# Tokens gathered in quarter rows and transposed on VectorE, with single-pass list products, in a fused delta-rule attention and expert kernel

## The chip, the core and the metric

The kernel runs on one core of a Trainium2 chip. Five engines work side by side, each through its own instructions in order: TensorE (PE in the profile, its weight loads as PEld), VectorE (DVE), ScalarE (ACT), GpSimd (POOL) and SyncE (SP), which here issues DMA transfers. GpSimd issues the indirect transfers, those whose rows are named by a list of indices. The metric is the device time of one execution in microseconds (us).

## The reference

A linear attention with the delta rule runs over 4 batches and 8 heads, 768 steps, 48 features. Its output, 3072 tokens of 8 x 48 = 384 features, is the input of a mixture of 8 experts: every token goes to the one expert with the highest logit, through two matrices (384 x 1024 and 1024 x 384) with a relu between, and is scaled by its softmax weight.

```python
for t in range(S):
    kt, vt, bt = (k_n[:, :, t], v[:, :, t], beta[:, :, t, None])
    y[:, :, t] = np.einsum('bhd,bhde->bhe', q[:, :, t], state)
    v_old = np.einsum('bhde,bhd->bhe', state, kt)
    state = state + bt[:, :, :, None] * np.einsum('bhd,bhe->bhde', kt, vt - v_old)
...
x = np.ascontiguousarray(attn_out.transpose(0, 2, 1, 3)).reshape(B * S, H * D)
...
logits = x @ w_gate + modality_bias[modality_id]
e_idx = np.argmax(logits, axis=1)
...
for e in range(E):
    mask = e_idx == e
    h = np.maximum(x[mask] @ w1[e], 0.0)
    out[mask] = gate_w[mask, None] * (h @ w2[e])
```

## The kernel before

**Two stages.** The attention stage takes about the first 265 us. Its order is written out by hand: a table of task numbers (`ORDER`, with `FILL`) says in which sequence the plan's tasks are issued, and each engine keeps that order. The attention output goes tile by tile (128 tokens x 384 features) into `xd` in device memory. The router's work and the first slot's loads are tasks of the same plan. Everything behind is written in the order of the program, and a scheduler of the framework, with its own costs, places it on each engine.

**Slots.** Tokens are sorted by expert into slots: a0 and a1 (512 tokens each, taken from the first 16 tiles of 128 tokens, so that they can start before the attention is done), b0, b1 and b2 (512 each, from all that is left), c0 and c1 (256) and e0 (128): 25 tiles. "Later slots" are a1 to e0, 21 tiles. Further slots stand behind a branch for inputs that need them. List a holds the token places of a0 and a1, list b those of the rest.

**Lists** (`Router.lists`, L675 to L710). For four token tiles at a time VectorE writes a one-hot matrix of a token's place within its group of 128 (L633) and a matrix of 0 or 1 that says in which group the token stands (L690), multiplied once by the gate weight (L691) and once by the token's number (L692). TensorE adds the products over all tiles (L698): 16 columns by group and kind for list a, 34 for list b. These are plain fp32 matmuls, which the profile records as two each. From the sums come the token numbers `gidx`, the gate weights and the output rows `sidx` (L700 to L710). List b is made while TensorE works on slots a0 and a1.

**A slot** has these steps. `weights`: eight loads by SP, four quarters of w1 and four of w2 (384 KB each, L793), into buffers that rotate. Each is split into a high part (ScalarE, L824) and a low part, the remainder (VectorE, L828). `tokens`, for each tile of 128: an indirect DMA on GpSimd brings 128 rows of 384 features (L797) into one of five buffers (tag "xs"), three TensorE transposes bring features onto partitions (L800), ScalarE writes the high part xh (L802) and VectorE the low part xl (L803). There is one xh and one xl for all slots: they can be written only when layer 1 of the slot before is done with them. `layer1` (L837): 72 products of 128 x 128 with up to 512 tokens (three terms: high by high, high by low, low by high), relu on ScalarE (L841), low part of h on VectorE (L843). `layer2` (L892): 24 products for each token tile, scaled by the gate on VectorE into one of three output buffers (L895), then an indirect DMA on GpSimd that scatters the 128 rows into the output (L896).

The program writes layer 1 of a slot, then loads and tokens of the next, then layer 2 of the slot; the scheduler mixes them. Tiles carry their slot's name: `xgb_0` is the gathered tile 0 of a b slot, `hpb` layer 1 and `opb` layer 2 of a b slot, `tpb` the sums of list b.

## Time and profile before

| | |
|---|---|
| runs shown | 508.93, 517.02, 517.77 us; median 517.02 |
| profiled execution | 507.84 us |
| its span in the profile | 506.1 us |
| mean granted TensorE clock | 0.944 |
| TensorE busy | 474.1 us (94%) |
| VectorE busy | 318.4 us (63%) |
| ScalarE busy | 200.2 us (40%) |
| GpSimd busy | 121.2 us (24%) |

The profile records one execution; busy time is the sum of an engine's instructions, and the granted clock is the share of full speed that TensorE was given. The span leaves out 1.7 us of the execution around it. Two of the three runs lie about 9 us above the third and the profiled one. In the rows quoted later, "L892 PE MATMUL out<-in" is an operation at line 892 on TensorE, "x16" is the number of records in a piece of the chain, and "[19.44 <-DVE tf2b L709]" is the idle time before it and what ended it.

### The profile page before, as it was taken

The page shows a single profiled execution, that of the slowest core. Times are in us where ns is not written, and L with a number is a line of the kernel's source. Part 1 is how long each engine was busy: PE and PEld are TensorE (multiplying, and loading weights), DVE is VectorE, ACT ScalarE, POOL GpSimd, SP SyncE. Part 2 cuts the span into 40 slices and gives each one's busy share as a digit, 9 for nine tenths or more (in the row PEclk, how much of TensorE's full clock was granted, in tenths as well). Part 3 has the DMA queues.
Part 4 walks back from the last instruction along what each step waited for, and adds up shares of the span by engine and source line. Part 5 has one row for each costly group of instructions (what it writes and reads, how often), then busy time and mean ns, then how long its engine had stood idle before and what let it go on. Part 6 is the DMA issues. An engine that isn't in the chain of part 4 may idle for free.

```text
span 506.1 us, 16393 instructions
## 1 busy us (share of the span) xinstructions
PE 474.1 (94%) x6973; PEld 433.2 (86%) x6973; DVE 318.4 (63%) x668; ACT 200.2 (40%) x396; POOL 121.2 (24%) x158
## 2 busy tenths in 40 slices
PE   6789999999998999899989999999999999999991
PEld 6689999998888888798977898898898898999991
DVE  2598645779788787495666787645355364447650
ACT  3413323536246573452552343224343333335540
POOL 9111420344512212103403020064133030020110
PEclk8589956999999999999989999999999999999996
DMA  8558203518776785575657215157326245146710
GB/s 287 184 148 236 65 3 96 146 55 272 273 198 153 218 279 178 151 213 170 184 181 245 67 62 188 62 157 228 101 94 209 73 139 162 45 132 208 252 64 8
DMA packets 81331, 78.27 MB, mean 155 GB/s; under 512 B 48041, under 2 KB 71607, under 8 KB 79968
## 3 DMA queue, kind: packets, MB, share of 16 engines
q1 hardware_dynamic: 78048, 67.49, 44.8%
q0 software_dynamic: 3200, 9.64, 5.7%
q8 instruction: 57, 0.93, 0.8%
q14 instruction: 26, 0.21, 0.1%
...
## 4 chain that ended last, share of the span: by engine, by line
PE 82%; DMA 6%; DVE 4%; issue 3%; ACT 2%; SPq 1%; POOL 0%; POOLq 0%; DVEq 0%; ACTq 0%
PE hpb L837 10%; PE opb L892 9%; PE opa L892 7%; PE hpa L837 5%; PE lv L390 5%; PE gp L184 4%; PE y L440 3%; PE hpc L837 3%; PE opc L892 3%; PE z L423 3%; PE S L429 3%; PE ks L417 3%; PE S L500 3%; PE y L437 2%; PE jo L314 2%
## 5 line engine op out<-in xcount | busy, mean ns | idle before, releaser
L892 PE MATMUL opb<-w2hb,h 128*128 128x384 f32 x192 | 52.8, 340 | 0.5 <-DVE oob L895 0.5
L843 DVE SCALAR_TENSOR_TENSOR h<-hpb,h 128x512 fp32r<-128x512 f32 x24 | 16.6, 691 | 41.5 <-ACT h L841 41.5
L837 PE MATMUL hpb<-xh,w1xb 128*128 128x512 f32 x144 | 40.7, 394 | 0.0
L892 PEld LDWEIGHTS opb<-w2hb,h 128*128 128x128 f32 x192 | 34.8, 188 | 1.8 <-DVE oob L895 1.0
L892 PE MATMUL opa<-w2ha,h 128*128 128x384 f32 x128 | 34.4, 343 | 0.0
L841 ACT ACTIVATE h<-hpb 128x512 fp32r<-128x512 f32 x24 | 14.4, 598 | 48.0 <-PE hpb L837 48.0
L892 PE MATMUL opb<-w2lb,h 128*128 128x384 f32 x96 | 32.5, 338 | 0.0
L837 PEld LDWEIGHTS hpb<-xh,w1xb 128*128 128x128 f32 x144 | 26.8, 188 | 4.5
L334 POOL TENSOR_TENSOR tmx<-T,A 128x456 f32<-128x456 f32 (+10 forms) x20 | 14.5, 725 | 65.3 <-DVE T L335 64.7
...
L419 DVE TENSOR_TENSOR RHS<-vv,ks 64x384 f32<-64x384 f32 x44 | 24.2, 551 | 4.7 <-PE ks L417 3.9
L500 PE MATMUL S<-ident 128*128 128x128 f32 x154 | 24.5, 304 | 1.5 <-DVE Sb L26 0.5
L896 POOL DMA_INDIRECT out_dram<-oob,sidxb x12 | 12.4, 1032 | 50.5 <-DVE oob L895 28.2
L25 ACT COPY ZT<-z 64x384 f32<-64x384 f32 x36 | 17.0, 473 | 17.3 <-PE z L423 16.8
L334 DVE TENSOR_TENSOR tmx<-T,A 128x396 f32<-128x396 f32 (+14 forms) x40 | 21.6, 539 | 3.6 <-POOL T L335 2.8
L440 PE MATMUL y<-ZT,pb 128*64 128x96 f32 x384 | 21.9, 259 | 2.0 <-DVE ZT L26 2.0
L892 PEld LDWEIGHTS opa<-w2ha,h 128*128 128x128 f32 x128 | 23.1, 188 | 0.8 <-DVE ooa L895 0.2
L500 PEld LDWEIGHTS S<-ident 128*128 128x128 f32 x154 | 21.0, 210 | 3.2 <-issue 0.7
L184 PE MATMUL gp<-kqr 48*64 48x64 f32 x896 | 17.6, 227 | 5.5 <-DMA kqr<-in_kq_dram 4.0
L423 PE MATMUL z<-RHS,R 128*64 128x96 f32 x384 | 22.2, 260 | 0.1
L335 DVE TENSOR_TENSOR T<-T,tmx 128x396 f32<-128x396 f32 (+14 forms) x40 | 21.2, 529 | 1.4
L892 PE MATMUL opa<-w2la,h 128*128 128x384 f32 x64 | 21.6, 337 | 0.0
...
## 6 DMA issues: line engine op xcount, KB each, us to landing
...
ke<-in_kq_dram SPq DMA_DIRECT2D x10, 512.0 KB, 7.6
...
```

Source lines behind the costliest of these rows:

```text
L25: if n=="scalar": nc.scalar.copy(o,i)
L184: s.I[f"g{c}"]=mm(t[k][o:o+64,64*(4*g+j):64*(4*g+j)+64],l,s.KQ[c][u:u+48,g,x,1] if a else l,start=True,stop=True)
L334: E[s.e].tensor_tensor(o,T[:,:,lo:lo+na,c:c+1].to_broadcast([128,n,na,nb]),X[:,:,c:c+1,c+1:32].to_broadcast([128,n,na,nb]),ALU.mult)
L335: x=T[:,:,lo:lo+na,c+1:32]; E[s.e].tensor_tensor(x,x,o,ALU.subtract)
L390: for p in range(2): b=64*p+32; x=2*j+h; mm(o[b-32:b+32,x],s.YS[i%2][b:b+32,x],R[b:b+32,x,32:64] if i>7 else w0(s.Wn[i//4],i)[b:b+32,4*h+j ...
L419: c,g=divmod(i,2); b=64*p; V.tensor_tensor(s.RHS[g][b:b+64,:,48*p:48*p+48].rearrange("q (h j) c -> q h j c",h=2),s.KV[c,1][b:b+64,g],s.ks[ ...
L423: for h in range(2): mm(s.z[i][64*h:64*h+64,:,j,:],s.R[i%4][:,2*j+h,:],hc(s.RHS[i%2][:,4*h+j,:]),start=True,stop=True)
L440: for p in range(2): mm(s.y[i][64*p:64*p+64,:,j,:],s.PB[i//2][:,8*(i%2)+4*p+j],hc(s.ZT[i%2][:,4*p+j,:]),start=(i<2 and j==0),stop=True,ski ...
L500: for _ in range(fill.get(t["k"],0)): s.nc.tensor.matmul(s.S[1][:,384:512],s.ident,s.ident,start=False,stop=True,skip_group_check=True)
L837: if n in ks: mm=s.nc.tensor.matmul(hp[:,v,:],w[:,k,fs],x[:,k,0:T],start=(n==0),stop=(n==8))
L843: s.nc.vector.scalar_tensor_tensor(hl,hp,0.0,hh.bitcast(F32),ALU.max,ALU.subtract)
L892: mm=nc.tensor.matmul(op,h[:,f%nf,ts_],w[:,f%2,:],start=(n==0),stop=(n==23)); n+=1
```

## The change

Four things are changed.

**Gathers.** For later slots, one gather of 128 rows x 384 features becomes four of 128 rows x 96. `xd` is seen as 12288 rows of 96 features, and the row's index is 4 x token + quarter, with the quarter depending on the partition's group of 32 in a way that puts a token's quarter rows where the transposition wants them. These indices (`x4a`, `x4b`) are made with the lists. a0 keeps the old gather, though both kinds share the new function.

**Transposes.** For later slots VectorE transposes the gathered tile in blocks of 32 x 32 (`turnq`) into another of the five "xs" buffers, in place of three TensorE transposes into PSUM. Features stand on partitions in another order then, so w1 is loaded in that order: four transfers of 32 partitions for a quarter of w1 where one stood.

**Lists.** The list products are single-pass (F32R) with four kinds of column (token number, gate high part, gate low part, mask), 32 columns for list a and 68 for list b. VectorE makes one more product for every four tiles, the gate's split and some small tiles once, and the gate's sum. One more product on TensorE spreads the token numbers over the partitions for the quarter indices. It adds two tasks to the plan, so the numbers in `ORDER` from 888 on shift by two, and "887" becomes "887 888 889".

**Drain.** Behind a slot's last scatter GpSimd gets a drain instruction, ahead of what the scheduler places next.

```diff
-...788d 778 478 ... 885 808 479d 886 827 887 809 482 810...
+...788d 778 478 ... 885 808 479d 886 827 887 888 889 809 482 810...
...
+    def split(s,t0,t1):
+        V=s.nc.vector; g,h=(x[:,t0:t1] for x in (s.gt,s.gh))
+        V.tensor_copy(h.bitcast(F32R),g); V.tensor_tensor(g,g,h,ALU.subtract)
...
-                B=LB[:,z][:,0:H*2*NH].rearrange("q (h b n) -> q h b n",h=H,b=2)
+                B=LB[:,z][:,0:H*4*NH].rearrange("q (h b n) -> q h b n",h=H,b=4)
...
-                V.tensor_tensor(B[:,:,0],ids.unsqueeze(1).to_broadcast([128,H,NH]),bn(pi),ALU.is_equal)
-                G.tensor_tensor(B[:,:,1],B[:,:,0],bn(s.gt),ALU.mult)
-                V.tensor_tensor(B[:,:,0],B[:,:,0],bn(s.tid),ALU.mult)
+                V.tensor_tensor(B[:,:,3],ids.unsqueeze(1).to_broadcast([128,H,NH]),bn(pi),ALU.is_equal)
+                for x,y in ((1,s.gh),(2,s.gt),(0,s.tid)): G.tensor_tensor(B[:,:,x],B[:,:,3].bitcast(F32),bn(y),ALU.mult)
...
-        V.tensor_scalar(gidx,tk,-1.0,0.0,ALU.add,ALU.max)
-        V.tensor_copy(gate,tp[:,1])
+        tg=T([128,NH],"tz"); V.tensor_scalar(tg,tk,-1.0,0.0,ALU.add,ALU.max)
+        V.tensor_tensor(tm,tg.unsqueeze(1).to_broadcast([128,4,NH]),m4.unsqueeze(2).to_broadcast([128,4,NH]),ALU.mult)
+        yield "PE",.25
+        nc.tensor.matmul(r4.rearrange("q a b -> q (a b)"),Lr,tm.rearrange("q b n -> q (b n)"),start=not zeroed,stop=True,skip_group_check=True)
+        yield "DVE",2.0
+        V.tensor_scalar(s.places[u][:,4*o0:4*o0+4*NH].rearrange("q (n b) -> q b n",b=4),r4,4.0,s.qn,ALU.mult,ALU.add)
+        V.tensor_copy(gidx,tg)
+        V.tensor_copy(gate,tp[:,1]); V.tensor_tensor(gate,gate,tp[:,2],ALU.add)
...
-        getattr(s.nc,C.w_q).dma_start(w,(s.w1,s.w2)[l-1][bass.ds(S["e"],1),q].rearrange("o p k f -> (o p) k f"))
+        W=(s.w1,s.w2)[l-1] if l==2 or u=="a0" else s.w1q
+        if W is s.w1q:
+            for r in range(4): getattr(s.nc,C.w_q).dma_start(w[32*r:32*r+32],W[bass.ds(S["e"],1),q,r].rearrange("o j k f -> (o j) k f"))
+        else: getattr(s.nc,C.w_q).dma_start(w,W[bass.ds(S["e"],1),q].rearrange("o p k f -> (o p) k f"))
...
     def gather(s,S,t,xg):
-        s.nc.gpsimd.indirect_dma_start(xg,None,S["x"],bass.IndirectOffsetOnAxis(ap=S["gidx"][:,S["c0"]+t:S["c0"]+t+1].bitcast(U32),axis=0))
+        c=S["c0"]+t; G=s.nc.gpsimd; ix=lambda a,c: bass.IndirectOffsetOnAxis(ap=a[:,c:c+1].bitcast(U32),axis=0)
+        if S["u"]=="a0": G.indirect_dma_start(xg,None,S["x"],ix(S["gidx"],c)); return
+        for b in range(4): G.indirect_dma_start(xg[:,96*b:96*b+96],None,S["x"].rearrange("t (q f) -> (t q) f",q=4),ix(s.router.places[S["l"]],4*c+b))
...
+    def turnq(s,xg,xp): s.nc.vector.transpose(xp.rearrange("q k (b t) -> q b k t",b=4),xg.rearrange("q (b k j) -> q b k j",b=4,k=3))
...
-            xp=env["ps"].tile([128,3,128],F32,name=f"xp{u}_{t}",tag=env["xp"],bufs=env["xpb"])
-            s.turn(xg,xp); s.xhi(t,xp); s.xlo(t,xp)
+            xp=s.A.pa.tile([128,3,128],F32,name=f"xt{u}_{t}",tag="xs",bufs=5)
+            s.turnq(xg,xp); s.xhi(t,xp); s.xlo(t,xp)
...
         X.layer2(S,o[0],o[2],not more)
+        if more:
+            with tc.issue_after(X.put.ins): nc.gpsimd.drain()
```

GpSimd, from the last scatter of slot a0 (`ooa_3_...`) on: gathers of b0 and b1 (L797 before, L820 in the changed kernel) and scatters of a1 (L896, L920). Before:

```order
L896 DMA out_dram<-ooa_3_4993,sidxa 3072x384
L797 DMA xgb_0_5135<-xd,gidxb 128x384
L797 DMA xgb_1_5143<-xd,gidxb 128x384
L797 DMA xgb_2_5151<-xd,gidxb 128x384
L797 DMA xgb_3_5159<-xd,gidxb 128x384
L797 DMA xgb_0_5436<-xd,gidxb 128x384
L797 DMA xgb_1_5444<-xd,gidxb 128x384
L797 DMA xgb_2_5452<-xd,gidxb 128x384
L896 DMA out_dram<-ooa_0_5204,sidxa 3072x384
L896 DMA out_dram<-ooa_1_5234,sidxa 3072x384
```

The same place in the changed kernel; "x4" is the four quarters of a tile:

```order
L920 DMA out_dram<-ooa_3_5044,sidxa 3072x384
L820 DMA xgb_0_5199<-xd,x4b 128x96 x4
L920 DMA out_dram<-ooa_0_5272,sidxa 3072x384
L820 DMA xgb_1_5208<-xd,x4b 128x96 x4
L920 DMA out_dram<-ooa_1_5302,sidxa 3072x384
L820 DMA xgb_2_5217<-xd,x4b 128x96 x4
L920 DMA out_dram<-ooa_2_5332,sidxa 3072x384
L820 DMA xgb_3_5226<-xd,x4b 128x96 x4
L920 DMA out_dram<-ooa_3_5362,sidxa 3072x384
L820 DMA xgb_0_5517<-xd,x4b 128x96 x4
```

The four gathers of b0 stood in a row ahead of a1's scatters; now each tile's quarters are followed by a scatter of a1, and the gathers of b1 have moved behind all of them.

TensorE, from the product of the changed kernel's list b that makes the quarter indices (L716) on, in layer 2 of a1 (L916):

```order
L916 MATMUL opa_1_5277<-w2la_3_5159,h_4616 128x384
L716 MATMUL tpb<-l1b 128x68
L916 MATMUL opa_0_5247<-w2ha_3_5158,h_4616 128x384
L916 MATMUL opa_1_5277<-w2ha_3_5158,h_4616 128x384
L916 MATMUL opa_0_5247<-w2ha_3_5158,h_4617 128x384
L916 MATMUL opa_0_5247<-w2la_3_5159,h_4616 128x384
L916 MATMUL opa_1_5277<-w2ha_3_5158,h_4617 128x384
L916 MATMUL opa_1_5277<-w2la_3_5159,h_4616 128x384
L916 MATMUL opa_2_5307<-w2ha_0_5074,h_4518 128x384
```

Between L716 and the first product of layer 1 of b0 there are 54 matmuls of layer 2 of a1 and nothing else. Before, the transposes of b0 stood among these matmuls:

```order
L892 MATMUL opa_1_5209<-w2la_3_5107,h_4599 128x384
L800 MATMUL xpb_0_5137<-ident,xgb_0_5135 128x128 x3
L892 MATMUL opa_0_5179<-w2ha_3_5106,h_4600 128x384
L892 MATMUL opa_0_5179<-w2la_3_5107,h_4599 128x384
L892 MATMUL opa_1_5209<-w2ha_3_5106,h_4599 128x384
L800 MATMUL xpb_1_5145<-ident,xgb_1_5143 128x128 x3
```

They have left TensorE. Their place on VectorE, from the third scaled output of a1 (L919) on, among the low parts of w2 (L852) and of x (L827) for b0:

```order
L919 TENSOR_SCALAR ooa_2_5332<-opa_2_5307,gatea 128x384
L824 STREAM_TRANSPOSE xtb_0_5204<-xgb_0_5199 128x4x3x32
L852 TENSOR_TENSOR w2lb_0_5393<-w2rb_0_5191,w2hb_0_5392 128x768
L827 TENSOR_TENSOR xl<-xtb_0_5204,xh 128x3x128
L852 TENSOR_TENSOR w2lb_1_5421<-w2rb_1_5193,w2hb_1_5420 128x768
L852 TENSOR_TENSOR w2lb_2_5449<-w2rb_2_5195,w2hb_2_5448 128x768
L919 TENSOR_SCALAR ooa_3_5362<-opa_3_5337,gatea 128x384
L852 TENSOR_TENSOR w2lb_3_5477<-w2rb_3_5197,w2hb_3_5476 128x768
L824 STREAM_TRANSPOSE xtb_1_5213<-xgb_1_5208 128x4x3x32
L827 TENSOR_TENSOR xl<-xtb_1_5213,xh 128x3x128
```

Each transpose waits for the four quarters of its tile, and each low part for the high part that ScalarE makes of the transposed tile; what stands below in VectorE's order waits with them.

More of the change, by code (lines that the diff above doesn't have):

```diff
@@ L112, in __init__ @@
         s.kqr=[T(f"kqr{g}",[128,2048]) for g in range(2)]
-        s.cst=T("cst",[128,72])
+        s.cst=T("cst",[128,73])
         for c in range(4):
@@ L116, in __init__ @@
             if c==0: nc.sync.dma_start(s.cst,s.cst_in)
-        s.um=s.cst[:,0:64]; s.m0,s.m1,*s.mk=(s.cst[:,k:k+1] for k in range(64,70)); s.mB=[s.cst[:,k:k+1] for k in (70,71)]
+        s.um=s.cst[:,0:64]; s.m0,s.m1,*s.mk=(s.cst[:,k:k+1] for k in range(64,70)); s.mB=[s.cst[:,k:k+1] for k in (70,71)]; s.router.qn=s.cst[:,72:73]
         s.eps=T("eps",[128,1]); nc.vector.memset(s.eps,1e-30)
@@ L551, in __init__ @@
         G.tensor_scalar(s.edge[512],s.iot[:,1:7],512.0,None,ALU.mult); G.tensor_scalar(s.edge[256],s.iot[:,0:12],256.0,128.0,ALU.mult,ALU.add); G.memset(s.edge[128],0.0)
-        s.lo=T([128,NT],"rlo",I32); s.OH=T([128,NT,8],"OH"); s.r=T([128,NT],"rank"); s.gt=T([128,NT],"gtok")
+        s.lo=T([128,NT],"rlo",I32); s.OH=T([128,NT,8],"OH"); s.r=T([128,NT],"rank"); s.gt,s.gh=(T([128,NT],n) for n in ("gtok","ghi")); s.places={}
         s.F=T([128,8],"taken"); G.memset(s.F,0.0)
@@ L586, in mute @@
         d=copies.copy(s)
-        for n in ("nc","slot","L","LT","bt","em8","ones","tri","W","keep","OH","r","lo","gt","iot","tid","zero","F","edge"): setattr(d,n,Mute())
+        for n in ("nc","slot","L","LT","bt","em8","ones","tri","W","keep","OH","r","lo","gt","iot","tid","gh","ident","qn","zero","F","edge"): setattr(d,n,Mute())
+        d.places={}
         return d
@@ L755, in part_b @@
         s.experts("b",hi,C.SB,sei,pw)
-        s.pib=pi; s.rest=lambda bank: s.lists("r",24,pi,m+NE-s.nm,s.ids[:,s.nm:],s.nm,out,pw,bank[:,0:2*(m+NE-s.nm)].rearrange("q (a b) -> q a b",a=2),6,False)
-        yield from s.lists("b",24,pi,s.nm,s.ids[:,0:s.nm],0,out,pw,bank("tpb")[:,0:2*s.nm].rearrange("q (a b) -> q a b",a=2),6,False)
+        s.pib=pi; s.rest=lambda bank: s.lists("r",24,pi,m+NE-s.nm,s.ids[:,s.nm:],s.nm,out,pw,bank,6,False)
+        yield from s.lists("b",24,pi,s.nm,s.ids[:,0:s.nm],0,out,pw,bank("tpb"),6,False)
         s.experts("c",hi2,NS,sei2,pw)
@@ L787, in slot_of @@
     def slot_of(s,u,T,sei,col,gidx,c0,x,env):
-        return dict(u=u,T=T,c0=c0,env=env,gidx=gidx,x=x,W={1:[],2:[]},e=getattr(s.nc,C.w_q).value_load(sei[0:1,col:col+1],min_val=0,max_val=7))
+        return dict(u=u,T=T,c0=c0,env=env,gidx=gidx,l="a" if u[0]=="a" else "b",x=x,W={1:[],2:[]},e=getattr(s.nc,C.w_q).value_load(sei[0:1,col:col+1],min_val=0,max_val=7))
     def load(s,S,l,q):
@@ L895, in layer2 @@
             nc.vector.tensor_scalar(oo,op,gate[:,c:c+1],None,ALU.mult)
-            nc.gpsimd.indirect_dma_start(s.out,bass.IndirectOffsetOnAxis(ap=sidx[:,c:c+1].bitcast(U32),axis=0),oo,None,bounds_check=3071,oob_is_err=False)
+            s.put=nc.gpsimd.indirect_dma_start(s.out,bass.IndirectOffsetOnAxis(ap=sidx[:,c:c+1].bitcast(U32),axis=0),oo,None,bounds_check=3071,oob_is_err=False)
 @with_exitstack
@@ L919, in tile_kernel @@
     env=dict(ps=pm,xp="mo",xpb=2,hp="mo",hpb=2,op="mo",opb=2)
-    A.X=X=Experts(tc,w1,w2,out,ident,slot,A); A.places=pa; A.sea=sea; A.prt=prt; A.first=(*f[0],env)
+    A.X=X=Experts(tc,w1,w2,out,ident,slot,A); X.router=R; A.places=pa; A.sea=sea; A.prt=prt; A.first=(*f[0],env)
     last=A.emit()
```

72 lines of the change are left out of this document (40 added, 32 removed).

## The prediction

> **What bounds the kernel now.** I read the page's first table, then the engines' busy time in windows of the expert stage, then the waits of TensorE there, the chain of waits around the second slot, and last GpSimd's own timeline.
>
> ```profile
> span 506.1 us, 16393 instructions
> PE 474.1 (94%) x6973; PEld 433.2 (86%) x6973; DVE 318.4 (63%) x668; ACT 200.2 (40%) x396; POOL 121.2 (24%) x158
> 260.00:305.00 45.00, 44.31 (x285) 38.72 (x282) 34.07 (x107) 18.91 (x31) 7.04 (x6) 0.98 0.42 133
> 305.00:345.00 40.00, 40.00 (x228) 36.55 (x227) 24.02 (x59) 12.66 (x20) 12.40 (x12) 1.00 0.42 132
> 380.00:415.50 35.50, 35.24 (x182) 31.73 (x181) 17.13 (x25) 12.70 (x21) 7.84 (x8) 1.00 0.43 134
> PE hp L837 <- DVE xl L803: 0.7, 1, 0.7
> PE opb L892 <- DVE oob L895: 0.5, 2, 0.3
> ```
>
> The window rows give length, then busy time of PE, PEld, DVE, ACT and POOL, then the granted clock. From 260 us on TensorE is never short of work: its longest waits are the last two rows, below 1 us each. So in this stage a matmul taken away shortens the kernel one for one, as long as what replaces it arrives in time, and every wait that is put before a layer lengthens it one for one. GpSimd has room (7.84 of 35.5 us). The chain says where the slots meet:
>
> ```profile
> 311.44 1.71 PE tpb L698 x16
> ...
> 325.51 1.71 PE tpb L698 x16
> 327.22 2.18 PE hpa L837 x9
> 329.40 4.41 PE opa L892 x25
> 333.81 0.33 PE xpb L800 x3
> ...
> 340.36 4.21 PE opa L892 x24
> 344.57 4.18 PE hpb L837 x18
> 328.43 0.99 POOL L797 DMA_INDIRECT xgb<-xd,gidxb  x1 [19.44 <-DVE tf2b L709]
> 334.12 0.95 POOL L797 DMA_INDIRECT xgb<-xd,gidxb  x1 [0.30 <-issue]
> 335.37 0.95 POOL L797 DMA_INDIRECT xgb<-xd,gidxb  x1 [0.30 <-PE opa L892]
> 337.88 1.02 POOL L896 DMA_INDIRECT out_dram<-ooa,sidxa  x1 [0.30 <-issue]
> L797 POOL DMA_INDIRECT xgb<-xd,gidxb x12: 944/967/1576, 328.4 to 371.0; - x12
> DMA to landing us min/median/max: 3.0/3.7/5.8
> 327.26 0.18 DVE L700 COPY tkb<-tpb 128x17 f32<-128x17 f32 x1 [1.09 <-PE tpb L698]
> ```
>
> Three pairs of batches of list b, 1.71 us each, lie on TensorE before 327.22. The list ends with small VectorE operations that start at 327.26, and at 328.43 GpSimd, which had been waiting for them 19.44 us, starts slot b0's gathers. The transposes L800 are fitted between matmuls of layer 2 of a1, and layer 1 of b0 starts at 344.57 with no gap. So 16 us lie between the first possible gather of b0 and the layer that needs all four of its tiles. In these 16 us GpSimd needs 1.25 us for each gather (334.12 to 335.37: 0.95 and 0.30 between).
>
> **The change part by part.**
>
> *Transposes leave TensorE.* 333.81 shows a tile's three transposes: 0.33 us. Later slots have 21 tiles: 6.9 us, of which a1's four take 1.3, b0's four 1.3, and the 13 behind b0 4.3. All lies on the saturated engine, so it is a gain of its full size where x comes in time.
>
> *VectorE takes them over.*
>
> ```profile
> L316 DVE STREAM_TRANSPOSE Wt<-A 128x256 f32<-128x256 f32 x8 | 3.5, 443 | 6.2 <-PE lv L384 6.1
> L294 DVE STREAM_TRANSPOSE W<-T 128x512 f32<-128x512 f32 x2 | 2.1, 1042 | 0.0
> L803 DVE TENSOR_TENSOR xl<-xpb,xh 128x384 fp32r<-128x384 f32 x12 | 6.2, 548 | 0.0
> L802 ACT CAST xh<-xpb 128x384 fp32r<-128x384 f32 x12 | 5.4, 482 | 10.3 <-PE xpb L800 10.3
> ```
>
> A tile of 384 columns lies between 0.443 us (256) and 1.042 us (512); I take 0.75. That is 3.0 us for each slot of 512 on an engine busy 17.13 of 35.5 us: hidden, except where it stands in line ahead of the h and w2 low parts, which I price below.
>
> *The lists.* List b is 48 records in 3 x 1.71 = 5.13 us. Single-pass products make it 24, plus one product (L716 of the changed kernel). At the present 1.71/16 = 0.107 us each, 25 take 2.7 us: 2.4 us less. The bounds are half of that (twice as many columns in half the time: a gain of 3.8 us) and 0.214 us (one single-pass product as dear as two records: -0.2 us). List a:
>
> ```profile
> 220.00:230.00 10.00, 10.00 (x233) 9.16 (x230) 8.62 (x38) 5.05 (x14) 0.96 (x2) 1.00 0.80 236
> 231.58 0.19 DVE L691 TENSOR_TENSOR l1a<-l1a,gtok 128x32 f32<-128x32 f32 x1
> ```
>
> There TensorE may save up to 2 us (32 records halve), but VectorE, busy 8.62 of 10 us, gets about ten small operations more (0.19 each: some 2 us). I count the two as zero, with 2 us to either side.
>
> *Quarter gathers, the largest term.* In the changed order the last list product stands 54 layer-2 matmuls ahead of layer 1 of b0. Without a stall that layer would start at 344.57 - 1.3 (transposes of a1) - 1.3 (of b0) - 2.4 (list) = 339.5. The 54 matmuls take 54 x 4.21/24 = 9.5 us, so the product runs at 330.1 and the first gather can start at 330.6 (its index needs one VectorE operation more). GpSimd's order is now: four quarters of tile 0, a scatter of a1, four quarters of tile 1, a scatter, and so on. A quarter still moves 128 rows, only shorter ones. No row shows the price of that. If it goes by rows it stays 1.25 us; if by bytes, 0.95/4 + 0.30 = 0.54 us; the dearest gather of the twelve took 1.58 + 0.30 = 1.88 us. I take 1.25, because the scatters (1.02 at 337.88) and gathers, which go opposite ways with the same 128 rows, already cost the same. Then the sixteenth quarter is issued at 330.6 + 15 x 1.25 + 3 x 1.32 = 353.3. It lands 3.7 us later, 357.0; transpose and high part add 0.75 + 0.48: layer 1 of b0 starts at 358.2. That is 13.7 us later than 344.57, and TensorE has nothing else in its order for about 19 us.
>
> A page of the Trainium skill weighs against this pricing, "DMA: Bandwidth & Descriptors", section "Anatomy of one DMA — SWDGE (gpsimd) path": each such transfer has a fixed cost of about 2.0 us whatever its bytes, mostly the receipt of the last byte. If quarters paid that one behind the other, the sum would be an estimated 15 x (2.0 - 1.25) = 11 us higher; the trace has gathers issued 1.25 us apart that land 3.7 us later, so receipts overlap here.
>
> *The clock after the gap.*
>
> ```profile
> 258.56 1.40 PE L440 MATMUL y<-ZT,pb 128*64 128x96 f32 x16 [1.97 <-DVE ZT L26]
> 260.00:265.00 5.00, 5.00 (x61) 4.04 (x58) 2.59 (x6) 4.54 (x7) 0.00 (x0) 0.78 0.63 201
> 500.00:506.00 6.00, 0.00 (x0) 0.00 (x0) 0.00 (x0) 0.00 (x0) 0.00 (x0) 0.50 0.00 1
> ```
>
> A busy window of 5 us just behind a gap of 1.97 us was granted 0.78: 1.1 us lost. At the end, with nothing to do, the clock stands at 0.50. A gap of 19 us ends at 0.50 too; I take 1.5 us lost, between 1.1 and 2.5 (five us at half). The skill's page "TensorE: Matmul & The Clock Gate", section "Why this matters for your kernels", asks for no gaps above some 3 us, since an idle window halves the clock; by its warm-up of about 3.4 us the loss would be an estimated 1.7 us, and the 0.50 row agrees.
>
> *Behind b0.* A slot of 512 tokens costs GpSimd 16 x 1.25 + 4 x 1.32 = 25 us, below the 35 us that its layers take on TensorE, so it catches up. But the gathers of a fourth tile wait for buffers that come free only when the slot before has left x, and scatters queue behind them; the scatters hold the three output buffers, and VectorE, in order, waits for one with h queued behind. With the VectorE transposes I price this at 1.5 us in all (0 to 5; nothing if scatters stay ahead). The 13 tiles give 4.3 us back.
>
> *With one answer:*
>
> ```profile
> L793 SPq DMA_DIRECT2D w1rb<-in_moe_w_dram x12: 372/373/692, 302.7 to 382.1; - x12
> ```
>
> w1 in four loads of 32 rows is 12 more issues a slot, 12 x 0.37 = 4.5 us on SP: hidden by the 35 us of a slot; if not, x waits anyway. The drain stands behind a slot's last scatter, ahead of the next gathers: nothing if it waits for issue alone, one landing (3.7 us) on GpSimd if for the data, which the later slots hide. For a1 itself there is no stall:
>
> ```profile
> 269.10 0.94 POOL L797 DMA_INDIRECT xga<-xd,gidxa  x1 [18.61 <-PE lg L575]
> 291.00 4.04 PE opa L892 x23
> ```
>
> Its second gather starts at 269.10, when buffers come free; twelve quarters of 1.25 from there end at 284.1, and 3.7 to land makes 287.8. Its layer 1, now in order right behind the 23 matmuls at 291.00, cannot start before 295.0; x is still read by layer 1 of a0 up to 291.0, and one high part and four low parts (0.48 + 4 x 0.55) fit in the 4 us between.
>
> *Sum*, against the profiled execution's 507.84 us: +13.7 (b0 late) +1.5 (clock) +1.5 (queues) -4.3 (later transposes) = 520.2, +2.4%. The runs shown lie 1 to 10 us above the profiled execution:
>
> ```profile
> 60.00:85.00 25.00, 25.00 (x467) 23.87 (x464) 11.47 (x29) 9.03 (x24) 4.42 (x7) 0.52 0.07 13
> ```
>
> This early stretch runs at a clock of 0.52, which may come and go between executions, so I add 3 us for a time to report: 523.
>
> **The rivals.**
>
> *Quarters go by bytes.* With 0.54 us a quarter the sixteenth is issued at 330.6 + 8.1 + 4.0 = 342.7, and layer 1 of b0 starts at 347.6, 3.1 later than before. With 1.1 for the clock and -4.3 the sum is 507.7: no change. For it: a quarter is a quarter of the data. Against it: gathers and scatters cost the same, though their data go different ways.
>
> *The gathers are hidden: the other side.* If x of b0 is there by 339.5, nothing stalls and all 4 gains count: 507.84 - 5.0 - 4.3 = 498.5, and with the list bound of 3.8 and list a's 2 down to 495.1. From 330.6 to 339.5 there are 8.9 us; 4.9 go to the landing, transpose and high part of the last tile, so 4.0 are left for fifteen quarters and the scatters between. It decides at a price of a quarter below 0.27 us, scatters set aside, or at a first gather 18.7 us (358.2 - 339.5) earlier. For it: the 0.30 between issues alone would almost do, if the 0.95 is nearly all data; and list products that run ahead of layer matmuls would bring the gather forward. Against it: 0.95 us at 334.12 is GpSimd's own busy time, and its order puts three scatters of 1.3 us into the same stretch, each behind its layer-2 tile.
>
> *Quarters are dearer than whole gathers.* At 1.88 us each the sixteenth is issued at 330.6 + 28.2 + 4.0 = 362.8 and layer 1 starts at 367.7, 23.1 later; a slot then costs GpSimd 16 x 1.88 + 5.3 = 35.4 us, as much as TensorE needs, so it becomes the bound. Sum: 507.84 + 23.1 + 1.5 + 1.5 - 4.3 = 529.6, more if the gathers lag further. For it: 16 outstanding transfers on one queue, which the trace never has. Against it: only one of twelve took so long.
>
> *The drain waits for data.* Then each slot's first gather comes 3.7 us later; between a1 and b0 it stands behind b0's gathers and costs nothing, later it uses up cover: 520.2 + 3 = 523, and with the 3 us above 526.
>
> **How the numbers follow.** Forecast 0.50 (516 to 530); quarters by bytes 0.18 (507 to 511); hidden 0.17 (495 to 502); dearer 0.08 (529 to 540); drain 0.07 (523 to 528). The range 500 to 532 leaves out most of the hidden case and the upper part of the dearer one, some 0.18. About 2% is what a measurement of this kernel can tell from no change; 2% of 507.84 is 10 us. Faster by more: two thirds of the hidden case, 0.12. Slower by more: the forecast from 518 up, 0.40 of its 0.50, the dearer case and half of the drain's, 0.52. Within: 0.36.
>
> **What would show it.** In the changed profile: a wait of TensorE in layer 1 of b0 for xh or xl, of 15 to 20 us, at about 340, with a clock near 0.5 behind it; GpSimd busy without a pause from 331 to 355 with starts 1.25 us apart (0.54 or 1.9 for the rivals); list b below 3 us on TensorE; transposes on VectorE near 0.75 us; no wait above 1 us at the later slots' layer 1. Wrong it is if that wait is below 5 us, if the slots behind b0 wait as well, or if the attention stage, up to 260 us, ends at another time than before by more than 2 us.

## The result, and the profile after

The changed kernel takes 529.37 us (median of 6 executions, 524.49 to 540.5), the kernel before 516.08 us (507.44 to 528.25). The ratio is 1.039, with a 95% interval of 1.030 to 1.049: slower by 3.9%. The ratio compares the executions within 1.5% of the fastest of their kernel, five of the changed one and two of the one before; the medians of all six lie 2.6% apart. Its profiled execution took 527.13 us, 19.3 us more than the 507.84 of before.

Executions of one kernel differ by 10 to 20 us, most of it in the attention stage, where the granted clock falls to about 0.5 for a stretch of changing length (a0 starts between 267 and 298 us in the profiles below). So times of stages are compared here, each from one profile: from the first product of a0 to the first of b0, from there to the first of c0, from there to the last product of the program, and the rest of the span, called the tail. Two kernels with the same work in the stages (before, and before with one instruction kind added, below) agree in them to 0.2 us. Two kernels that were profiled twice repeat less well (b0 to c0 took 124.6 and 107.5 us in one, a0 to b0 107.7 and 97.2 in the other), so 1 or 2 us between single profiles show little.

| stage (us) | before | changed | difference |
|---|---|---|---|
| start to a0 | 267.1 | 267.5 | +0.4 |
| a0 to b0 | 77.3 | 90.4 | +13.1 |
| b0 to c0 | 96.0 | 105.7 | +9.7 |
| c0 to last product | 54.7 | 55.2 | +0.5 |
| tail | 11.0 | 6.6 | -4.4 |
| span | 506.1 | 525.4 | +19.3 |

The first rows of the changed kernel's page, with the sums of the engines:

```profile
span 525.4 us, 16665 instructions
PE 468.9 (89%) x6872; PEld 425.8 (81%) x6872; DVE 332.5 (63%) x717; ACT 199.9 (38%) x396; POOL 187.3 (36%) x221
```

The waits of its TensorE behind 230 us (total, times, longest):

```profile
PE hpb L861 <- ACT xh L826: 17.7, 1, 17.7
PE hpb L861 <- DVE h L867: 3.9, 2, 2.9
PE opb L916 <- DVE oob L919: 2.6, 1, 2.6
```

TensorE has 5.2 us less to do, as the change intends, and is kept waiting. The 17.7 us stand ahead of slot b0. GpSimd's timeline there, with the first quarter, the second and the sixteenth:

```profile
330.83 0.99 POOL L820 DMA_INDIRECT xgb<-xd,x4b  x1 [19.03 <-DVE gateb L720]
332.12 0.97 POOL L820 DMA_INDIRECT xgb<-xd,x4b  x1 [0.30 <-issue]
...
354.08 0.94 POOL L820 DMA_INDIRECT xgb<-xd,x4b  x1 [0.30 <-issue]
```

And the first products of b0 in TensorE's timeline:

```profile
357.91 2.93 PE L861 MATMUL hpb<-xh,w1xb 128*128 128x512 f32 x6 [17.66 <-ACT xh L826]
```

A quarter gather costs GpSimd the same 0.95 us and 0.30 between as a whole one did; sixteen of them and three scatters take from 330.83 to 355.02. Part of the wait lies ahead of them. VectorE's timeline, with the token numbers of list b (all that a whole gather needs) and the quarter indices:

```profile
326.39 0.17 DVE L719 CAST gidxb<-tzb 128x17 int32<-128x17 f32 x1
330.23 0.33 DVE L718 TENSOR_SCALAR x4b<-tpb,cst 128x68 int32<-128x68 f32 x1
```

The indices come 3.84 us behind the token numbers, since the added product (L716, at 329.89) stands between them.

The smaller waits stand in b1 and b2. VectorE's timeline there, with what it waited for in brackets:

```profile
391.46 0.58 DVE L824 STREAM_TRANSPOSE xtb<-xgb 128x384 f32<-128x384 f32 x1 [3.44 <-DMA xgb<-xd,x4b]
...
397.73 0.58 DVE L824 STREAM_TRANSPOSE xtb<-xgb 128x384 f32<-128x384 f32 x1 [4.13 <-DMA xgb<-xd,x4b]
398.23 1.78 DVE L852 TENSOR_TENSOR w2lb<-w2rb,w2hb 128x768 fp32r<-128x768 f32 x2
399.94 0.61 DVE L919 TENSOR_SCALAR oob<-opb,gateb 128x384 f32<-128x384 f32 x1
400.46 0.95 DVE L852 TENSOR_TENSOR w2lb<-w2rb,w2hb 128x768 fp32r<-128x768 f32 x1
401.33 1.28 DVE L867 SCALAR_TENSOR_TENSOR h<-hpb,h 128x512 fp32r<-128x512 f32 x2
```

TensorE's timeline, three of its pauses:

```profile
400.60 0.44 PE L916 MATMUL opb<-w2hb,h 128*128 128x384 f32 x1 [2.58 <-DVE oob L919]
402.07 1.65 PE L861 MATMUL hpb<-xh,w1xb 128*128 128x512 f32 x3 [1.03 <-DVE h L867]
440.23 1.65 PE L861 MATMUL hpb<-xh,w1xb 128*128 128x512 f32 x3 [2.91 <-DVE h L867]
```

Windows around them (length, busy time of PE, PEld, DVE, ACT, POOL, granted clock):

```profile
400.00:407.00 7.00, 5.37 (x17) 4.36 (x18) 4.03 (x8) 0.60 (x1) 5.20 (x6) 0.76 0.88 218
439.00:448.00 9.00, 7.77 (x23) 6.60 (x24) 3.88 (x6) 0.60 (x1) 4.45 (x5) 0.62 0.68 181
```

At 397.73 a transpose for the next slot ends a wait of 4.13 us for its quarters. Behind it in VectorE's order stand the low parts of w2, the scaled output that frees the buffer TensorE needs (400.60) and the h that it needs next (402.07). Behind such a pause of 2.6 to 3 us the granted clock is 0.76 and 0.62, so that nine products of b1 take 3.86 us instead of 2.08. The totals of VectorE's waits for the gathers' data, from 345 to 460 us in the changed kernel:

```profile
DVE xtb L824 <- DMA xgb<-xd,x4b: 30.0, 10, 4.3
DVE xtc L824 <- DMA xgc<-xd,x4b: 3.8, 3, 2.7
```

Of the 30.0 us, 19.1 lie behind the first product of b0.

The tail is shorter. At the program's end GpSimd issues drains of its own, and an instruction that counts up the semaphores of its transfers (columns: count, shortest/median/longest in ns). First before, then the changed kernel, then the changed kernel without its drains (an experiment below):

```profile
L954 POOLq INC_SWDGE_SEM  x1: 1188/1188/1188, 499.9 to 499.9; - x1
L980 POOLq DRAIN  x3: 40/107/4162, 501.1 to 505.9; - x3
```

```profile
L980 POOLq INC_SWDGE_SEM  x1: 203/203/203, 523.6 to 523.6; - x1
L1006 POOLq DRAIN  x3: 46/107/130, 523.9 to 525.1; - x3
L972 POOLq DRAIN  x7: 2822/4886/7174, 310.1 to 512.4; - x7
```

```profile
L978 POOLq INC_SWDGE_SEM  x1: 2448/2448/2448, 536.1 to 536.1; - x1
L1004 POOLq DRAIN  x3: 40/107/9307, 538.6 to 548.4; - x3
```

The last drain takes 4.16 us behind 50 indirect transfers and 9.31 behind 113: some 0.08 us for each. Drains in between leave 0.13 us. Their own records last 2.8 to 7.2 us (L972), partly beside transfers that GpSimd still issues: the one from 352.2 to 358.8 us overlaps the gather at 354.08.

The other terms of the prediction, in the groups of instructions: VectorE's transpose of a tile, and the products of list b.

```profile
L824 DVE STREAM_TRANSPOSE xtb<-xgb 128x384 f32<-128x384 f32 x12 | 6.9, 579 | 33.5 <-DMA xgb<-xd,x4b 30.5
L710 PE MATMUL tpb<-l1b,l0b 128*128 128x68 f32 x24 | 3.1, 260 | 0.0
```

### The profile page after: what moved, and what is told of

Read it like the earlier page. It is cut to its first block, busy times and chain, and to the rows that moved or that the text cites. A ratio compares the mean times of both kernels' runs of the same rounds, so it can differ in the third digit from the quotient of the medians.

```text
span 525.4 us, 16665 instructions
## 1 busy us (share of the span) xinstructions
PE 468.9 (89%) x6872; PEld 425.8 (81%) x6872; DVE 332.5 (63%) x717; ACT 199.9 (38%) x396; POOL 187.3 (36%) x221
## 5 line engine op out<-in xcount | busy, mean ns | idle before, releaser
L861 PE MATMUL hpb<-xh,w1xb 128*128 128x512 f32 x144 | 44.6, 424 | 21.6 <-ACT xh L826 17.7
L820 POOL DMA_INDIRECT xgb<-xd,x4b x48 | 48.8, 1016 | 39.2 <-DVE gateb L720 19.0
L916 PE MATMUL opb<-w2hb,h 128*128 128x384 f32 x192 | 53.4, 342 | 2.8 <-DVE oob L919 2.6
L861 PEld LDWEIGHTS hpb<-xh,w1xb 128*128 128x128 f32 x144 | 29.0, 206 | 27.7 <-ACT xh L826 18.0
L916 PEld LDWEIGHTS opb<-w2hb,h 128*128 128x128 f32 x192 | 35.7, 191 | 4.7 <-DVE oob L919 2.9
L916 PE MATMUL opa<-w2ha,h 128*128 128x384 f32 x128 | 34.5, 340 | 0.4 <-DVE ooa L919 0.4
L867 DVE SCALAR_TENSOR_TENSOR h<-hpb,h 128x512 fp32r<-128x512 f32 x24 | 16.2, 681 | 27.1 <-ACT h L865 27.1
L916 PE MATMUL opb<-w2lb,h 128*128 128x384 f32 x96 | 32.7, 341 | 0.0
L25 ACT COPY Sb<-S 48x192 f32<-48x192 f32 x68 | 21.3, 313 | 18.0 <-PE S L429 13.1
L824 DVE STREAM_TRANSPOSE xtb<-xgb 128x384 f32<-128x384 f32 x12 | 6.9, 579 | 33.5 <-DMA xgb<-xd,x4b 30.5
L820 POOL DMA_INDIRECT xga<-xd,x4a x16 | 17.6, 1099 | 19.5 <-PE lg L575 14.9
L916 PEld LDWEIGHTS opa<-w2ha,h 128*128 128x128 f32 x128 | 23.2, 188 | 1.2 <-DVE ooa L919 0.7
L25 ACT COPY ZT<-z 64x384 f32<-64x384 f32 x36 | 17.0, 473 | 18.2 <-PE z L423 17.7
```

The source lines that it names most:

```text
L25: if n=="scalar": nc.scalar.copy(o,i)
L820: for b in range(4): G.indirect_dma_start(xg[:,96*b:96*b+96],None,S["x"].rearrange("t (q f) -> (t q) f",q=4),ix(s.router.places[S["l"]],4* ...
L861: if n in ks: mm=s.nc.tensor.matmul(hp[:,v,:],w[:,k,fs],x[:,k,0:T],start=(n==0),stop=(n==8))
L867: s.nc.vector.scalar_tensor_tensor(hl,hp,0.0,hh.bitcast(F32),ALU.max,ALU.subtract)
L916: mm=nc.tensor.matmul(op,h[:,f%nf,ts_],w[:,f%2,:],start=(n==0),stop=(n==23)); n+=1
```

## The experiments

Theory A: GpSimd's price per gather makes both losses, the one ahead of b0 and those behind. Theory V: the VectorE transposes, in one line with h and the scaled outputs, make those behind b0. Rivals L (lists), D (drain) and S (SP's loads) are tried beside them. Stage times of all runs, in us:

| kernel | a0 to b0 | b0 to c0 | c0 to last product | tail |
|---|---|---|---|---|
| before | 77.3 | 96.0 | 54.7 | 11.0 |
| changed | 90.4 | 105.7 | 55.2 | 6.6 |
| whole gathers | 73.9 | 99.6 | 54.4 | 6.6 |
| whole gathers, no drain | 73.8 | 100.3 | 54.6 | 10.9 |
| whole gathers, w1 in one load | 73.6 | 98.0 | 54.3 | 6.6 |
| halves | 74.6 | 108.3 | 54.6 | 6.6 |
| b0 as before | 73.6 | 107.0 | 54.8 | 7.0 |
| b0 as before, no drain (first, second) | 77.8, 73.6 | 124.6, 107.5 | 54.1, 56.8 | 16.3, 16.2 |
| changed, no drain | 90.6 | 100.2 | 54.3 | 17.5 |
| transposes behind h (first, second) | 107.7, 97.2 | 128.8, 128.5 | 51.5, 51.7 | 6.8, 6.8 |
| lists and drain | 74.3 | 95.8 | 54.9 | 6.7 |
| drain alone | 77.1 | 96.0 | 54.7 | 6.5 |
| lists alone | 74.3 | 96.3 | 54.9 | 11.1 |
| lists, drain, a1 as changed | 77.1 | 95.8 | 55.0 | 6.6 |
| lists and drain, clean | 74.7 | 96.0 | 55.4 | 6.5 |

**One whole gather a tile.**

```diff
-        for b in range(4): G.indirect_dma_start(xg[:,96*b:96*b+96],None,S["x"].rearrange("t (q f) -> (t q) f",q=4),ix(s.router.places[S["l"]],4*c+b))
+        G.indirect_dma_start(xg,None,S["x"],ix(S["gidx"],c))
```

> The changed kernel, but a later slot's tile is brought by one gather of 128 whole rows instead of four of quarter rows; everything else (VectorE transposes, w1 in four loads, lists, drain) stays, so features land in other places than the product needs and only the time is read. Theory A (GpSimd's price per gather, about 1.25 us whatever its bytes, makes both losses): the wait of layer 1 of b0 (17.7 us) falls below 1 us, the pauses in layer 1 of b1 and b2 (2.6, 1.0, 2.9 us) go with it, time 497 to 502 us, which is the price forecast for the hidden rival. Theory V (the VectorE transposes in one line with h and the output scaling, and the buffers shared by gather and transpose, cost time of their own): the first wait goes, but pauses of 2 to 4 us stay in b1 and b2, time 508 to 513 us.

Measured: 510.98 us median (504.95 to 514.62) beside 517.5 of before; the ratio is 0.983 (0.973 to 0.993). The wait ahead of b0 is gone (73.9 us), as A says. The run takes two things away at once, though, twelve of b0's sixteen gathers and the wait for the quarter indices. By the timelines above the twelve make 15.0 us (1.25 each) and the indices 3.84, together somewhat over the 17.7 us of the wait; no run separates them. But from b0 to c0 it took 99.6 us, not the 92.7 that are left when ten tiles' transposes (0.33 us each) leave TensorE. TensorE still paused four times for h, 5.5 us in all. So behind b0 theory V holds a share that A doesn't explain. The stage from b0 to c0 as one window: before, changed, whole gathers.

```profile
344.41:440.45 96.04, 95.53 (x484) 85.25 (x483) 45.40 (x64) 34.40 (x55) 18.52 (x19) 1.00 0.43 136
357.91:463.64 105.73, 98.96 (x457) 86.97 (x457) 49.26 (x75) 33.96 (x54) 61.88 (x60) 0.94 0.40 111
351.06:450.61 99.55, 93.61 (x457) 82.29 (x457) 51.73 (x78) 34.82 (x55) 23.62 (x21) 1.00 0.47 135
```

TensorE stands idle for 0.5, 6.8 and 5.9 us (length less busy time). So quarters wait only 0.8 us longer than whole gathers here. The other 5.4 of the 6.2 us between these two are busy time for the same 457 records, at a granted clock of 0.94 instead of 1.00.

The expectation names the buffers that gather and transpose share, and the record shows them at work: a transposed tile keeps one of the five "xs" buffers until its low part is made. GpSimd's gathers of the second and the fourth tile of b2 before the change, then of the second with whole gathers:

```profile
353.80 0.99 POOL L797 DMA_INDIRECT xgb<-xd,gidxb  x1 [0.30 <-issue]
371.02 0.94 POOL L797 DMA_INDIRECT xgb<-xd,gidxb  x1 [14.96 <-PE xpb L800]
```

```profile
380.13 1.02 POOL L820 DMA_INDIRECT xgb<-xd,gidxb  x1 [13.78 <-DVE xl L827]
```

Before, the second tile was gathered 9.4 us behind the first product of b0, and only the fourth waited long. With whole gathers the second waits 13.78 us for the low parts of the slot before and comes 29.1 us behind that product, so that its transpose stands in VectorE's line with scaled outputs and h behind it. No run gives the transposed tiles buffers of their own; how the loss behind b0 divides between the buffers and VectorE's order stays open.

**The old tokens, with the new lists and the drain.**

```diff
-        W=(s.w1,s.w2)[l-1] if l==2 or u=="a0" else s.w1q
+        W=(s.w1,s.w2)[l-1] if l==2 or u[0] in "abcept" else s.w1q
...
-        if S["u"]=="a0": G.indirect_dma_start(xg,None,S["x"],ix(S["gidx"],c)); return
+        if S["u"][0] in "abcept": G.indirect_dma_start(xg,None,S["x"],ix(S["gidx"],c)); return
...
-            s.turnq(xg,xp); s.xhi(t,xp); s.xlo(t,xp)
+            if u[0] in "abcept":
+                xp=env["ps"].tile([128,3,128],F32,name=f"xp{u}_{t}",tag=env["xp"],bufs=env["xpb"]); s.turn(xg,xp)
...
+            s.xhi(t,xp); s.xlo(t,xp)
```

> The changed kernel with gathers, transposes and w1 loads of every slot as they were before; new are the lists and the drain alone. Theory A: the lists give their 2.4 us and the drain costs nothing, time 504 to 507 us beside 508 before. Rival L (the lists cost as much on VectorE as they save on TensorE): 508 or more.

Measured: 515.45 us median beside 517.5, ratio 0.994 (0.988 to 1.001), not to be told from no change by its total. In its profile, a0 to b0 is 3.0 us shorter than before and the tail 4.3 shorter. Rival L finds nothing in the expert stage; what the list of a costs ahead of a0 is hidden by that stretch's own spread.

**b0 alone the old way**; its transposes and w1 loads go by the same condition.

```diff
-        if S["u"]=="a0": G.indirect_dma_start(xg,None,S["x"],ix(S["gidx"],c)); return
+        if S["u"] in ("a0","b0"): G.indirect_dma_start(xg,None,S["x"],ix(S["gidx"],c)); return
```

> The changed kernel with slot b0 alone handled as before (four whole gathers, TensorE transposes, one w1 load each); a1, b1, b2, c0, c1, e0 are as changed. Theory A: without b0's sixteen quarters GpSimd has no backlog, b1 and b2 get their tiles in time, and the time is 500 to 505 us. Theory V: the first loss (13.5 us and 1.4 of clock) goes, the 11 us in b1 and b2 stay, time 511 to 515 us.

Measured: 525.58 us median (519.52 to 532.24) beside 517.5 of before. The first loss is gone (73.6 us), the second isn't (107.0): A's forecast of 500 to 505 falls; V's comes closer, but even the fastest execution lies above its 515. TensorE's pauses and VectorE's wait for the data of the gathers:

```profile
PE hpb L864 <- DVE h L870: 8.3, 3, 3.0
DVE xtb L824 <- DMA xgb<-xd,x4b: 17.8, 6, 5.7
```

Three pauses of 2.6 to 3.0 us, one for each slot, and the clock behind them (0.63 to 0.79 in windows of 7 to 8 us) are the loss. So a backlog of GpSimd left by b0 is not needed for it.

**No drain.**

```diff
-        if more:
-            with tc.issue_after(X.put.ins): nc.gpsimd.drain()
```

> The changed kernel without the drain behind each slot. Theory A: the drain ends in GpSimd's gap of 3.2 us ahead of b1's first quarter and in nothing else; time within 2 us of the changed kernel's 528. Rival D (the drain holds GpSimd until data has landed and so makes the backlog behind b0): 518 to 522 us, without the pauses of b1 and b2.

Measured: 546.84 us median (538.89 to 550.51) beside 517.5 of before; the ratio is 1.049 (1.038 to 1.061). Neither expectation holds. From b0 to c0 it took 100.2 us, 5.5 less than with the drain, but the tail grew from 6.6 to 17.5: the 9.31 us drain shown above. That led to theory T.

**The drain alone, on the kernel before.**

```diff
         X.layer2(S,o[0],o[2],not more)
+        if more:
+            with tc.issue_after(X.put.ins): nc.gpsimd.drain()
```

> The kernel before with one edit: the drain behind each slot's last scatter. What is new since the last runs is theory T: at the end of the program GpSimd clears up after every indirect transfer since its last drain, 1.19 us and 4.16 us in the profile of before, 2.45 and 9.31 in the kernel without the drain, 0.20 and 0.13 with it; drains behind the slots move this into time that GpSimd has free. Theory T: the stretch from the last product to the end falls from 11.0 to 6.7 us, the expert stage stays at 228 us, time 4 us (0.9%) below before. Rival D (the drain holds up the next slot's gathers): the stage grows by 3 to 6 us and eats that.

Measured: stages as before to 0.2 us, the tail 6.5 instead of 11.0: in the profile T is right, and rival D finds nothing where tiles are gathered whole. The total did not show it: the ratio is 1.006 (0.998 to 1.013), which leaves out the 0.9% forecast. Why 4.5 us of the profile don't come out in the total stays open; its profile starts a0 at 272.0 instead of 267.1.

**The lists alone.**

> The kernel before with the new lists alone, no drain. The lists' term: the stage from the first product of a0 to the last product falls from 228.0 to 225.0 us as in the run with lists and drain; the stretch behind it stays at 11 us; time 2.4 to 3 us (0.6%) below before. Rival L: what VectorE does more in the attention stage moves the start of a0 by 2 us or more, and the time is that of before.

Measured (the edit is the lists' part of the diff above, on the kernel before): ratio 1.000 (0.995 to 1.004). a0 to b0 is 3.0 us shorter, the tail 11.1; the start of a0, 276.8 in this profile, takes more than the gain. With a spread of some 10 us there, whether the list of a costs 2 us can't be said from it.

**The change for a1 alone, with lists and drain**; the transposes and w1 loads go by the same condition.

```diff
-        if S["u"]=="a0": G.indirect_dma_start(xg,None,S["x"],ix(S["gidx"],c)); return
+        if S["u"]!="a1" and S["u"][0] in "abcept": G.indirect_dma_start(xg,None,S["x"],ix(S["gidx"],c)); return
```

> New lists and drain, and the quarter gathers, VectorE transposes and w1 quarter loads for slot a1 alone; b0 to e0 as before. Theory A and the term for a1 of 1.3 us: the stage is 223.7 us, and with the drain's 4 us and the lists' 3 the time is 8 us (1.6%) below before. Theory V (VectorE's line costs a1 as well): a pause of 1 to 3 us in layer 1 of a0 or a1, stage 226 us or more.

Measured: ratio 0.996 (0.991 to 1.001). a0 to b0 took 77.1 us, 2.8 more than with a1's tiles the old way, of which one pause has 1.36 us; another part is a clock of 0.66 in the first 5 us of a0, which is not a1's doing. No gain of 1.3 us is seen.

**Transposes behind h**, so that no h can wait for them.

```diff
-            s.turnq(xg,xp); s.xhi(t,xp); s.xlo(t,xp)
+            with s.tc.issue_after(s.lasth.ins) if u[0] in "abce" else contextlib.nullcontext(): s.turnq(xg,xp)
+            s.xhi(t,xp); s.xlo(t,xp)
```

> The changed kernel, with one order changed: a slot's VectorE transposes stand behind the last low part of h of the slot before, so that no h can wait behind a transpose whose quarters have not landed. Theory V: the pauses for h in b1 and b2 (2.6, 1.0 and 2.9 us and the halved clock behind them) go; from the first product of b0 to the first of c0 it takes 93 to 97 us where the changed kernel takes 105.7. Theory A: GpSimd's quarters are late anyway, waits for x of 4 to 6 us at the start of b1 and b2 take the place of the pauses, and it takes 101 to 106 us. Both: the wait of 17 us ahead of b0 stays.

> The kernel whose VectorE transposes stand behind the last h of the slot before, once more, since its one profile had waits of 10 us for nothing that the profile names. Theory A: waits for x of 5 to 10 us ahead of b1 and b2 come again, 105 us or more from the first product of b0 to the first of c0. If they were that execution's alone: 93 to 100 us.

Measured: 594.68 us in one execution, then 565.65 (median of 2), ratio 1.097 (1.079 to 1.115). Both took 128.5 to 128.8 us from b0 to c0. The pauses for h are gone; in the second, waits of 5.6 to 9.9 us for x stand ahead of b0, b1, b2 and c0 instead, so theory A's forecast for this order came, and more of it. The 17 us ahead of b0, which both expected to stay, became 9.8 in the second, but list b's products waited 10.5 us for VectorE. GpSimd's timeline of the second shows why:

```profile
389.98 0.94 POOL L820 DMA_INDIRECT xgb<-xd,x4b  x1 [0.30 <-issue]
406.88 1.08 POOL L921 DMA_INDIRECT out_dram<-oob,sidxb  x1 [15.95 <-DVE oob L920]
408.26 0.98 POOL L820 DMA_INDIRECT xgb<-xd,x4b  x1 [0.30 <-issue]
...
428.16 1.02 POOL L921 DMA_INDIRECT out_dram<-oob,sidxb  x1 [0.30 <-issue]
```

With one tile's quarters issued, GpSimd stands 15.95 us before a scatter whose output VectorE has not made, because layer 2 has not begun; the other twelve quarters come behind it. So the order of the transposes is not free: earlier they hold up h, later their gathers fall behind scatters, and twelve quarters do not fit into layer 2.

**Whole gathers without the drain.**

> One whole gather for each later tile instead of four quarters (features land in other places than the product needs, only the time is read), and no drain. It tells the drain from VectorE's order behind b0. In the run with whole gathers and drain it took 99.6 us from the first product of b0 to the first of c0, where the transposes taken away would leave 92.7. Theory D2 (the drain holds GpSimd for 3 to 7 us just when the next slot's tiles are due): 93 to 95 us here, no pause above 1 us. Theory V (the transposes ahead of h in VectorE's order cost it whatever GpSimd does): 98 to 100 us, the pauses stay.

Measured (both edits above together; one execution, 531.04 us): 100.3 us from b0 to c0, with pauses of 2.98, 1.02 and 1.02 us for h. This is 0.3 us above V's forecast, and D2 falls for whole gathers.

**b0 as before, no drain**, twice.

> Slot b0 as before, the other later slots as changed, and no drain. With the drain it took 107.0 us from the first product of b0 to the first of c0, with pauses of 2.6, 3.0 and 2.8 us. Theory D2: without it the pauses go, 94 to 97 us. Theory A (GpSimd's sixteen quarters for each slot are too slow by themselves, drain or not): 100 us or more, with pauses of 2 to 3 us left.

> The kernel with b0 as before and no drain, once more, since in its one profile the loads of w2 landed 10 us late from no cause that the profile names. If that came from this kernel (SP's w1 loads among GpSimd's gathers), it takes 120 us or more again from the first product of b0 to the first of c0, with waits of 6 to 10 us for w2. If it was that execution alone: 95 to 102 us, theory D2 below 97, theory A above 100.

Measured: the first (one execution, 570.21 us) took 124.6 us from b0 to c0, with waits of 10.2, 6.7 and 7.5 us behind late weights; the second (528.32 us, median of 2) 107.5 with pauses of 3.2, 3.0 and 2.8 us, beside 107.0 with the drain. So those weights were late in that execution alone, and here the drain costs the slots nothing. Its 5.5 us in the changed kernel rest on one pair of profiles.

**Two halves a tile.**

```diff
-        for b in range(4): G.indirect_dma_start(xg[:,96*b:96*b+96],None,S["x"].rearrange("t (q f) -> (t q) f",q=4),ix(s.router.places[S["l"]],4*c+b))
+        for b in range(2): G.indirect_dma_start(xg[:,192*b:192*b+192],None,S["x"].rearrange("t (q f) -> (t q) f",q=2),ix(S["gidx"],c))
```

> The changed kernel with two gathers of half rows for a later tile in place of four quarters (features land in other places than the product needs, only the time is read). A dose for the price of a gather: from the first product of a0 to the first of b0 it took 73.9 us with one gather a tile and 90.4 with four. If a gather costs GpSimd 1.25 us whatever its bytes, the eighth is issued at 330.6 + 7 x 1.25 + 1.3 on the clock of the changed kernel's trace and b0 starts 6.1 us late: 80 us. If it goes by bytes (0.95/2 + 0.30 = 0.78): 76.7 us.

Measured (one execution, 526.66 us): a0 to b0 took 74.6 us, less than either figure. The price is the expected one, though:

```profile
339.14 0.99 POOL L820 DMA_INDIRECT xgb<-xd,gidxb  x1 [11.82 <-DVE gidxb L719]
340.43 0.97 POOL L820 DMA_INDIRECT xgb<-xd,gidxb  x1 [0.30 <-issue]
341.70 0.95 POOL L820 DMA_INDIRECT xgb<-xd,gidxb  x1 [0.30 <-issue]
```

A half costs 1.27 us from start to start like a quarter and a whole row. But this kernel gathers by token number, which is ready 3.4 us ahead of the product that spreads the numbers (339.14 beside 342.52), and the time between hides the eight. As a dose for the first wait the run is spoiled by that. From b0 to c0 it took 108.3 us, more than quarters (105.7) and whole gathers (99.6), so the second loss does not follow the number of gathers.

**Whole gathers, w1 in one load.**

```diff
-        W=(s.w1,s.w2)[l-1] if l==2 or u=="a0" else s.w1q
+        W=(s.w1,s.w2)[l-1]
```

> One whole gather a tile, VectorE transposes and drain, and w1 in one load for each quarter of it as before (features and rows of w1 don't match, only the time is read). It took 99.6 us from the first product of b0 to the first of c0 with w1 in four loads, where 92.7 would be left with the transposes taken away. Theory V (transposes, output scaling and h in VectorE's one line, scatters and gathers in GpSimd's): 98 to 101 us again. Rival S (SP's sixteen issues hold up w2's loads behind them): 93 to 96 us.

Measured (one execution, 502.97 us): 98.0 us from b0 to c0, pauses of 2.2, 1.0 and 1.0 us. V again; by this pair of profiles at most 1.6 us of the 99.6 belong to SP's sixteen issues. VectorE's waits in it:

```profile
DVE xtb L824 <- DMA xgb<-xd,gidxb: 10.2, 6, 2.5
```

Counted alike, for `xtb` and `xtc` from the first product of b0 to the first of c0, VectorE waits 22.9 us for gathered data in the changed kernel, 22.5 with halves, 17.4 with quarters and no drain, 16.9 with one whole gather and 14.9 here. There is no such wait in the kernel before, whose VectorE has no operation that waits for a gather.

**A version that beats both**: single-pass lists and the drain on the kernel before, without the quarter indices.

```diff
-                B=LB[:,z][:,0:H*2*NH].rearrange("q (h b n) -> q h b n",h=H,b=2)
+                B=LB[:,z][:,0:H*4*NH].rearrange("q (h b n) -> q h b n",h=H,b=4)
...
+        if more:
+            with tc.issue_after(X.put.ins): nc.gpsimd.drain()
```

> The kernel before with the single-pass list products and the drain alone; no quarter indices, so one product of TensorE and some small VectorE operations less than in the run of lists and drain together. Stage from the first product of a0 to the last product 225 us (before: 228), the stretch behind it 6.7 us (before: 11.0); time 7 us (1.4%) below before if the attention stage is untouched. Rival L (the list of a costs VectorE more in the attention stage than TensorE saves): the start of a0 is later by 2 us or more on average, and the gain is below 1%.

Measured: 512.39 us median (508.12 to 522.24) beside 518.81 of before in the same session, ratio 0.989 (0.980 to 0.997): faster by 1.1%, which is below 2%. The stages add to 226.1 us (before 228.0) and the tail is 6.5. Neither part showed a gain of the total by itself (1.000 and 1.006), and its profile starts a0 at 286.3 us, so rival L can't be judged.

## Why the prediction was right or wrong

The direction was right, and the size was not: 520.2 us was forecast for the profile's own execution, +12.4, and it took +19.3.

- **b0 late, +13.7.** Right in mechanism and number. The first quarter was issued at 330.83 (forecast 330.6), the sixteenth at 354.08 (353.3), the first product of b0 ran at 357.91 (358.2). The sixteenth came 0.8 us late and landed 1.0 early (2.66 us beside the 3.7 assumed), which is luck. Bytes do not set GpSimd's price: it is 1.25 us with a quarter, half or whole row, always for 128 rows. The starts 1.25 us apart show it as the main cause; the whole-gather run agrees, but takes away the wait for the indices as well. The rivals "by bytes", "hidden" and "dearer" fall with this price.
- **The clock behind the gap, +1.5.** Right: six products took 2.93 us where six of the same kind take 1.53 without a gap (at 385.10 us), 1.4 us lost.
- **Transposes off TensorE, -4.3 behind b0.** They are gone, but with whole gathers TensorE's busy time from b0 to c0 is only 1.9 us less (93.61 beside 95.53), where ten of the thirteen tiles were to give 3.3. They were no gain: from a0 to the last product it took 227.9 us with whole gathers (225.9 with w1 in one load) and 225.0 with the old tokens.
- **Queues behind b0, +1.5 (0 to 5).** This is the step that failed. From b0 to the end of c0's stage the difference is +9.7 and +0.5. With the 4.3 us of transposes (as forecast) and 1.4 us of clock set apart, 13.1 us were lost there, nearly nine times the value and over twice the upper end. I had named the place (VectorE in one line, with h behind, and buffers that hold back a fourth tile) and priced it as if GpSimd's free time per slot, 35 less 25 us, were cover. It isn't: the quarters are spread over the slot between scatters that wait for VectorE, and VectorE stands in its order before transposes that wait for the quarters. With whole gathers the buffers hold back the second tile already. Slots b1 and b2 each pay a pause of 2.6 to 2.9 us and then the clock, which I had counted only behind the long gap. Waits of TensorE give 6.8 us in the b slots (2.58 + 1.03 + 2.91 + 0.25) and 1.8 in the c slots, products at the lower clock some 4.6 (3.86 us for 2.08 at 402, 5.93 for 3.13 at 440): together 13.2, or 12.2 without the 1.0 us that the kernel before waits there too.
- **The drain, at nothing.** It shortened the tail by 4.4 us, which I had not seen coming. So the sum is 6.9 us below the measured one because 11.6 us are missing on one side and 4.4 + 0.3 on the other; that it missed by no more is luck. What the drain costs the slots stays open: without it b0 to c0 was 5.5 us shorter in one pair of profiles, and 0.5 and 0.7 longer in two others.
- **The lists, -2.4.** Right: 24 products of 3.1 us in all where 48 records took 5.6, and a0 to b0 2.6 to 3.0 us shorter in the three runs that have the lists without the quarters.
- **No stall for a1, w1's loads hidden.** No wait of TensorE above 0.4 us stands in layer 1 of a1. But the 2.6 us that the transposes of a1 and b0 were to give did not come: a0 to b0 took 73.9 us with whole gathers, 0.4 less than with the old tokens (74.3). Of w1's loads at most 1.6 us can be told.
- **What would show it.** "No wait above 1 us at the later slots' layer 1" was the sign that came out against the prediction, and so did its "if the slots behind b0 wait as well"; both pointed to the right step.

The pages cited stand so. On "TensorE: Matmul & The Clock Gate" of the Trainium skill, section "Why this matters for your kernels", the table asks for no gaps above about 3 us: here pauses of 2.58 and 2.91 us already went with windows at 0.76 and 0.62, while one of 2.81 us with whole gathers and one of 1.62 us with halves went with 1.00. On "DMA: Bandwidth & Descriptors" of the Trainium skill, section "Anatomy of one DMA — SWDGE (gpsimd) path", a fixed cost of some 2 us, mostly the receipt, did not queue up: quarters were issued 1.25 us apart, each landing a median of 2.8 us later.
